# Ordering a recurrence's matmuls kind by kind over two batches: reads of both, values of both, state sums of both

## The chip, the cores and the metric

The kernel runs on one core of a Trainium2 chip. The metric is device time in microseconds (us), the median of several executions. TensorE multiplies matrices, VectorE, ScalarE and GpSimd do elementwise work, and SyncE issues the transfers. A ratio below is the mean time of one kernel's runs over the mean of the other's from the same rounds, so it is not quite the ratio of the medians quoted beside it.

## The reference

Four batches of eight heads go through a retention recurrence over 768 time steps; the result is the input of a two-layer network.

```python
gamma = 1.0 - 2.0 ** (-5.0 - np.arange(H))            # B, H, S, D = 4, 8, 768, 64
for t in range(S):
    state = gamma * state + outer(k[:, :, t], v[:, :, t])
    y[:, :, t] = scale * q[:, :, t] @ state
x = y.transpose(0, 2, 1, 3).reshape(B * S, H * D)     # 3072 x 512
h = x @ w_in                                          # 512 -> 2048
out = np.maximum(0.01 * h, h) @ w_out                 # 2048 -> 512
```

## The kernel before

The recurrence runs in six chunks of 128 steps. For one chunk and one batch there are two stages. The first makes the *scores* (keys against queries, `ap`), which VectorE masks. The second, shown here, has three kinds of product in one pair of PSUM banks: **reads** (queries against the state carried in), **values** (masked scores against values) and **state sums** (keys against values, for the next chunk). VectorE then drains the banks and updates the state.

```python
def stage_y(c, b, xb):                                # chunk c, batch b
    x, y = heads.pop((c, b)); ks, vs = y[:, 0], y[:, 1]
    am = scores.pop((c, b))
    ps = two_banks(f"yp_{c}_{b}")                     # 2 such buffers, shared with the scores
    pairs = [(j, m, i) for m in range(HP // 2) for j in range(2) for i in range(2)]   # eight
    if c > 0:
        for j, m, i in pairs:                         # reads: 64 rows x 64 columns of the array
            nc.tensor.matmul(ps[ts(i, 64), j, m, :], lhsT=st[b][ts(j, 64), 2 * m + i, :],
                             rhs=x[ts(j, 64), 0, 2 * m + i, :], start=(m == 0), stop=False, ...)
    for j, m, i in pairs:                             # values: 128 rows x 64 columns
        nc.tensor.matmul(ps[ts(i, 64), j, m, :], lhsT=vs[:, ...], rhs=am[:, j, 2 * m + i, :], ...)
    if more:                                          # state sums: 128 rows x 64 columns
        ...
    nc.vector.tensor_tensor(out=blocks, in0=ps[:, :, 0 : HP // 2, :], in1=gq, op=ALU.mult)  # drain
    if more:
        ...                                           # two VectorE operations: the new state
    load(...)                                         # the batch after the next
```

Around it lie the products of the feed-forward part (seven block products M1 to M7 in place of eight). In chunks 0 and 1 the batches are scored and read one by one, while the weights are still being loaded and rounded. In chunks 2 to 5 two batches are scored together behind one feed-forward product and read together three products later:

```python
at = {1: [scored(c + 1, u), scored(c + 1, u + 1)],
      4: [read(c + 1, u), read(c + 1, u + 1)]}
run(hidden(c, u, *xs[c], *pair[-1][1:]), at)
```

## Time and profile before

| | before |
|---|---|
| median of the first 3 runs | 688.67 us (688.64 to 690.79) |
| span of the profile | 686.5 us |
| TensorE busy | 663.5 us, 97% |
| VectorE, ScalarE, GpSimd busy | 55%, 24%, 4% |
| a paired stage with sums, without (chunk 5) | 4.17 us, 3.24 us |

A matmul's end in this profile is modelled and matmuls overlap. So "97% busy" says that TensorE nearly always has something running, not how fast. What a stretch of matmuls costs is read from the starts: from the first start of one stretch to the first start of the next. The prediction shows the lines.

### The profile page before, as it was taken

What the parts mean: (1) busy time and instruction counts of PE and PEld (TensorE: products, weight loads), DVE (VectorE), ACT (ScalarE), POOL (GpSimd) and SP (SyncE); (2) the same over time, 40 slices, a digit from 0 to 9 for tenths busy, and PEclk for the clock granted to TensorE, in tenths of its full rate; (3) what the DMA queues carried; (4) which work ended last, traced back from release to release, by engine and by line L of the source; (5) the groups of instructions that cost most, each with busy time, mean ns of one, the idle gap of its engine ahead of it and who ended that gap; (6) DMA issues with size and microseconds to landing.
All of it is one profiled execution on the core that took longest, in us unless ns stands there. A gap on an engine that the chain in (4) does not pass through costs nothing.

```text
span 686.5 us, 9550 instructions
## 1 busy us (share of the span) xinstructions
PE 663.5 (97%) x4096; PEld 578.9 (84%) x4096; DVE 375.6 (55%) x573; ACT 166.8 (24%) x275; POOL 28.0 (4%) x29
## 2 busy tenths in 40 slices
PE   5787999999999999999999999999999999999997
PEld 5676888888888888888888888888888888888886
DVE  4878767988888765613653533553451354341342
ACT  4432455445543001311210221220221130221210
POOL 1110000000001010100100100100000000000000
PEclk9999999999999999999999999999999999999999
DMA  8741222223412453100301300301300000100001
GB/s 315 283 154 62 82 72 84 92 72 123 153 34 90 138 181 119 55 1 10 114 1 62 123 0 1 123 1 62 123 0 1 1 1 16 46 1 0 1 1 62
DMA packets 15162, 49.12 MB, mean 72 GB/s; under 512 B 1680, under 2 KB 1680, under 8 KB 15120
## 3 DMA queue, kind: packets, MB, share of 16 engines
q1 hardware_dynamic: 15120, 48.51, 20.2%
q8 instruction: 32, 0.52, 0.3%
q14 instruction: 10, 0.08, 0.0%
HBM read 42.21 MB, written 6.29 MB: 71 GB/s over the span
## 4 chain that ended last, share of the span: by engine, by line
PE 94%; DMA 3%; DVE 1%; issue 1%; POOL 0%; ACT 0%; SPq 0%; POOLq 0%
PE B_h L303 12%; PE A_o L303 12%; PE B_o L303 12%; PE C_o L303 12%; PE C_h L303 12%; PE A_h L303 12%; PE D_h L303 6%; PE D_o L303 6%; PE yp L150 3%; PE ap L126 3%; PE yp L145 1%; PE yp L158 1%; DMA qk<-in_qk_dram 1%; DMA raw<-in_weights_dram 1%; DMA kv<-in_kv_dram 1%
## 5 line engine op out<-in xcount | busy, mean ns | idle before, releaser
L303 PE MATMUL A_h<-x,win 128*128 128x256 f32 x384 | 91.0, 380 | 0.0
L303 PEld LDWEIGHTS A_h<-x,win 128*128 128x128 f32 x384 | 72.7, 190 | 10.0
L303 PE MATMUL A_o<-g,wout 128*128 128x256 f32 x288 | 68.2, 380 | 0.0
L318 ACT ACTIVATE g<-g 128x512 f32<-128x512 f32 x72 | 43.8, 630 | 86.0 <-DVE g L252 85.9
L303 PEld LDWEIGHTS A_o<-g,wout 128*128 128x128 f32 x288 | 54.6, 190 | 7.8 <-ACT g L333 0.4
L252 DVE TENSOR_TENSOR m<-m,B_h 128x512 f32<-128x512 f32 x24 | 16.5, 687 | 65.6 <-PE B_h L303 65.6
L252 DVE TENSOR_TENSOR m<-m,B_o 128x512 f32<-128x512 f32 x16 | 11.0, 686 | 66.1 <-PE B_o L303 66.1
L323 ACT COPY m<-A_h 128x512 f32<-128x512 f32 x24 | 14.1, 586 | 135.6 <-PE A_h L303 103.9
L112 POOL TENSOR_TENSOR kv<-kv,dec 128x512 f32<-128x512 f32 x24 | 27.5, 1145 | 470.3 <-DMA kv<-in_kv_dram 276.8
L303 PE MATMUL B_h<-t,win 128*128 128x256 f32 x192 | 45.5, 380 | 1.0 <-DVE t L255 1.0
L303 PE MATMUL C_h<-t,win 128*128 128x256 f32 x192 | 46.1, 383 | 0.0
L303 PE MATMUL B_h<-x,win 128*128 128x256 f32 x192 | 46.0, 382 | 0.0
L303 PE MATMUL D_h<-t,win 128*128 128x256 f32 x192 | 45.5, 380 | 0.0
L303 PE MATMUL C_h<-x,win 128*128 128x256 f32 x192 | 45.5, 380 | 0.0
L163 DVE TENSOR_TENSOR x<-yp,dec 128x512 f32<-128x512 f32 x24 | 16.6, 690 | 46.3 <-PE yp L158 33.4
L303 PEld LDWEIGHTS B_h<-t,win 128*128 128x128 f32 x192 | 36.4, 190 | 6.3 <-DVE t L255 1.4
L150 PE MATMUL yp<-am,kv 128*64 128x128 f32 x384 | 29.4, 301 | 12.1 <-issue 8.1
L303 PEld LDWEIGHTS D_h<-t,win 128*128 128x128 f32 x192 | 36.4, 190 | 5.0
L303 PEld LDWEIGHTS C_h<-x,win 128*128 128x128 f32 x192 | 36.4, 190 | 5.0
L303 PEld LDWEIGHTS C_h<-t,win 128*128 128x128 f32 x192 | 35.9, 190 | 5.4
L303 PEld LDWEIGHTS B_h<-x,win 128*128 128x128 f32 x192 | 36.0, 190 | 5.3 <-issue 0.3
L255 DVE TENSOR_TENSOR gd<-g,gd 128x512 f32<-128x512 f32 x48 | 36.8, 767 | 1.6
(88 smaller groups left out, 1006.8 us busy)
## 6 DMA issues: line engine op xcount, KB each, us to landing
raw<-in_weights_dram SPq DMA_DIRECT2D x32, 512.0 KB, 3.8
qk<-in_qk_dram SPq DMA_DIRECT2D x24, 512.0 KB, 4.8
kv<-in_kv_dram SPq DMA_DIRECT2D x24, 512.0 KB, 5.5
out_dram<-o SPq DMA_DIRECT2D x24, 256.0 KB, 2.1
dec<-decay_dram SPq DMA_DIRECT2D x1, 262.0 KB, 5.5
```

Source lines behind the costliest of these rows:

```text
L112: nc.gpsimd.tensor_tensor(out=v, in0=v, in1=gk.unsqueeze(2).to_broadcast([128, H, D]), op=ALU.mult)
L126: nc.tensor.matmul(ps[:, j, a, :], lhsT=x[ts(j, 64), 1, a, :], rhs=x[ts(j, 64), 0, a, :])
L145: nc.tensor.matmul(ps[ts(i, 64), j, m, :], lhsT=st[b][ts(j, 64), a, :], rhs=x[ts(j, 64), 0, a, :], start=(m == 0), stop=False, skip_group_ ...
L150: nc.tensor.matmul(ps[ts(i, 64), j, m, :], lhsT=vs[:, 2 * a + j, :], rhs=am[:, j, a, :], start=(c == 0 and m == 0), stop=True, skip_group_ ...
L158: nc.tensor.matmul(sp[ts(j, 64), a, :], lhsT=ks[:, 2 * a + j, :], rhs=vs[:, 2 * a + j, :], start=False, stop=True, skip_group_check=True)
L163: nc.vector.tensor_tensor(out=blocks, in0=ps[:, :, 0 : HP // 2, :], in1=gq, op=ALU.mult)
L252: nc.vector.tensor_tensor(out=out, in0=a, in1=b, op=ALU.add)
L255: nc.vector.tensor_tensor(out=out, in0=a, in1=b, op=ALU.subtract)
L303: nc.tensor.matmul(ps[:, i, :], lhsT=block(w, sa)[:, k, ts(i, 128)], rhs=rhs[:, k, :], start=(first and i == 0 and n == 0 and k == 0), sto ...
L318: nc.scalar.activation(g[:, i], g[:, i], AF.Prelu, alpha=0.01)
L323: nc.scalar.copy(out=got["m1"], in_=ps)
```

## The change

The intent is to let products of one kind of both batches follow each other, so that TensorE meets fewer changes between kinds. The stage takes a tuple of batches. Its loops, cut to their order:

```diff
-    def stage_y(c, b, xb):
+    def stage_y(c, bs, xb):
+        got = [(b, *heads.pop((c, b)), scores.pop((c, b)), two_banks(f"yp_{c}_{b}")) for b in bs]
+        for b, x, _, _, ps in got:
             for ...:  # reads
+        for _, _, y, am, ps in got:
             for ...:  # values
+        for b, _, y, _, ps in got:
             for ...:  # state sums
+        for b, _, _, _, ps in got:
             # drain, state update, load
...
-                      3: [read(2, 2 * c), read(2, 2 * c + 1)]}
+                      3: [read(2, 2 * c, 2 * c + 1)]}
...
-                          4: [read(c + 1, u), read(c + 1, u + 1)]}
+                          4: [read(c + 1, u, u + 1)]}
```

Calls with one batch, in chunks 0 and 1, keep their order.

More of the change, by code (lines that the diff above doesn't have):

```diff
@@ L131, in stage_a @@
             in1=mask.unsqueeze(1).to_broadcast([128, H, C]), op=ALU.mult)
-    def stage_y(c, b, xb):
-        x, y = heads.pop((c, b))
-        ks, vs = y[:, 0], y[:, 1]
-        am = scores.pop((c, b))
-        ps = two_banks(f"yp_{c}_{b}")
-        pairs = [(j, m, i) for m in range(HP // 2) for j in range(2) for i in range(2)]
-        if c > 0:
-            for j, m, i in pairs:
-                a = 2 * m + i
+    def stage_y(c, bs, xb):
+        got = [(b, *heads.pop((c, b)), scores.pop((c, b)), two_banks(f"yp_{c}_{b}")) for b in bs]
+        more = c < NC - 1
+        pairs = [(j, m, i, 2 * m + i) for m in range(HP // 2) for j in range(2) for i in range(2)]
+        sums = {}
+        for b, x, _, _, ps in got:
+            for j, m, i, a in pairs if c > 0 else ():
                 nc.tensor.matmul(ps[ts(i, 64), j, m, :], lhsT=st[b][ts(j, 64), a, :],
@@ L147, in stage_y @@
                                  skip_group_check=True)
-        for j, m, i in pairs:
-            a = 2 * m + i
-            nc.tensor.matmul(ps[ts(i, 64), j, m, :], lhsT=vs[:, 2 * a + j, :],
-                             rhs=am[:, j, a, :], start=(c == 0 and m == 0), stop=True,
-                             skip_group_check=True)
-        more = c < NC - 1
-        if more:
-            sp = ps[:, 0, HP // 2 :, :].rearrange("p a (two d) -> p (a two) d", two=2)
-            for a in range(HP):
+        for _, _, y, am, ps in got:
+            for j, m, i, a in pairs:
+                nc.tensor.matmul(ps[ts(i, 64), j, m, :], lhsT=y[:, 1, 2 * a + j, :],
+                                 rhs=am[:, j, a, :], start=(c == 0 and m == 0), stop=True,
+                                 skip_group_check=True)
@@ L157, in stage_y @@
+        for b, _, y, _, ps in got:
+            sp = sums[b] = ps[:, 0, HP // 2 :, :].rearrange("p a (two d) -> p (a two) d", two=2)
+            for a in range(HP) if more else ():
                 for j in range(2):
-                    nc.tensor.matmul(sp[ts(j, 64), a, :], lhsT=ks[:, 2 * a + j, :],
-                                     rhs=vs[:, 2 * a + j, :], start=False, stop=True,
+                    nc.tensor.matmul(sp[ts(j, 64), a, :], lhsT=y[:, 0, 2 * a + j, :],
+                                     rhs=y[:, 1, 2 * a + j, :], start=False, stop=True,
@@ L160, in stage_y @@
                                      skip_group_check=True)
-        th, o = divmod(b * C, N)
-        blocks = xb.rearrange("p (kh th) k n -> p kh th k n", th=2)[:, :, th, :, ds(o, C)]
-        nc.vector.tensor_tensor(out=blocks, in0=ps[:, :, 0 : HP // 2, :], in1=gq, op=ALU.mult)
-        if more:
-            if c > 0:
-                nc.vector.tensor_tensor(out=st[b], in0=st[b], in1=sp, op=ALU.add)
-            nc.vector.tensor_tensor(out=st[b], in0=st[b] if c > 0 else sp,
-                                    in1=gc.unsqueeze(2).to_broadcast([128, HP, D]), op=ALU.mult)
@@ L169, in stage_y @@
-        n = c * B + b + AHEAD
-        if n < NC * B and n - 2 * B not in range(AHEAD):
-            load(*divmod(n, B))
+        for b, _, _, _, ps in got:
+            th, o = divmod(b * C, N)
+            blocks = xb.rearrange("p (kh th) k n -> p kh th k n", th=2)[:, :, th, :, ds(o, C)]
+            nc.vector.tensor_tensor(out=blocks, in0=ps[:, :, 0 : HP // 2, :], in1=gq, op=ALU.mult)
+            sp = sums[b]
+            if more:
+                if c > 0:
+                    nc.vector.tensor_tensor(out=st[b], in0=st[b], in1=sp, op=ALU.add)
+                nc.vector.tensor_tensor(out=st[b], in0=st[b] if c > 0 else sp,
+                                        in1=gc.unsqueeze(2).to_broadcast([128, HP, D]),
+                                        op=ALU.mult)
+            n = c * B + b + AHEAD
+            if n < NC * B and n - 2 * B not in range(AHEAD):
+                load(*divmod(n, B))
@@ L424, in scored, with read @@
         return do
-    def read(c, b):
-        return lambda: stage_y(c, b, xs[c][0])
+    def read(c, *bs):
+        return lambda: stage_y(c, bs, xs[c][0])
     def differ(c):
```

## The prediction

> **What bounds the kernel now.** I began with the page's first two parts, to see which engine sets the end.
>
> ```profile
> PE 663.5 (97%) x4096; PEld 578.9 (84%) x4096; DVE 375.6 (55%) x573; ACT 166.8 (24%) x275; POOL 28.0 (4%) x29
> ...
> PEclk9999999999999999999999999999999999999999
> ```
>
> TensorE is busy for 97% of 686.5 us at a clock that is nowhere throttled, and every other compute engine is under 60%. The chain that ended last says the same ("PE 94%; DMA 3%; DVE 1%"). So a change counts only if it alters the time TensorE needs, or makes it wait. The view of waits for TensorE says where it waits now:
>
> ```profile
> PE yp L150 <- issue: 8.1, 4, 4.6
> PE ap L126 <- DMA qk<-in_qk_dram: 5.7, 2, 4.6
> PE yp L150 <- POOL kv L112: 2.6, 2, 1.8
> PE yp L150 <- DVE am L129: 1.4, 1, 1.4
> PE B_h L303 <- DVE t L255: 1.0, 1, 1.0
> ```
>
> (Columns: total us, times, longest.) The same view restricted to 215 us onwards is empty: all these waits belong to the start, chunks 0 and 1, where the recurrence is done one batch at a time. The diff leaves those calls with one batch each, hence the same instructions. It pairs batches only in chunks 2 to 5, two pairs each: eight stages. In all eight TensorE waits for no other engine. Their durations come from the view by windows (us, then busy time of each engine):
>
> ```profile
> 229.68:233.85 4.17, 4.17 (x98) 3.69 (x97) 2.41 (x5) 0.00 (x0) 0.00 (x0) 1.00 0.54 150
> ...
> 433.37:437.55 4.18, 4.18 (x98) 3.70 (x97) 1.44 (x3) 0.60 (x1) 0.00 (x0) 1.00 0.47 136
> 488.27:491.52 3.25, 3.25 (x66) 2.56 (x65) 0.69 (x1) 0.60 (x1) 0.00 (x0) 1.00 0.45 141
> 542.24:545.49 3.25, 3.25 (x66) 2.56 (x65) 0.69 (x1) 0.60 (x1) 0.00 (x0) 1.00 0.00 0
> ```
>
> Six stages of 4.17 us and two of 3.25 us (chunk 5 has no state sums): 31.5 us, 4.6% of the span. That is all the change can work on. Inside one of them, the timeline (start, duration to the last end, engine, line, product, count):
>
> ```profile
> 433.37 0.67 PE L145 MATMUL yp<-qk,st 64*64 64x128 f32 x16
> 433.97 1.09 PE L150 MATMUL yp<-am,kv 128*64 128x128 f32 x16
> 434.90 0.63 PE L158 MATMUL yp<-kv 128*64 128x64 f32 x16
> 435.46 0.67 PE L145 MATMUL yp<-qk,st 64*64 64x128 f32 x16
> 436.06 1.09 PE L150 MATMUL yp<-am,kv 128*64 128x128 f32 x16
> 436.98 0.63 PE L158 MATMUL yp<-kv 128*64 128x64 f32 x16
> ```
>
> L145 is a state read (R), on a 64x64 corner of the array; L150 values (V) and L158 state sums (S) both use 128 rows and 64 columns. From start to start: R 0.60, V 0.92, S 0.56. The array changes shape at R to V and at S to R, but not at V to S. To price the seams I cut narrow windows around them:
>
> ```profile
> 433.75 0.29 PE L145 MATMUL yp<-qk,st 64*64 64x128 f32 x4
> 433.97 0.33 PE L150 MATMUL yp<-am,kv 128*64 128x128 f32 x2
> ...
> 435.30 0.23 PE L158 MATMUL yp<-kv 128*64 128x64 f32 x2
> 435.46 0.34 PE L145 MATMUL yp<-qk,st 64*64 64x128 f32 x4
> ```
>
> The last group of four reads starts at 433.75, the first pair of values 0.22 us later; the last pair of sums starts at 435.30, the next read 0.16 us later. (Reads start in fours within 0.02 us, values and sums in twos; I call these groups.) Inside a kind the instruction starts in the trace show 0.109 us from group to group for R and V, and 0.058 us for S. The first interval after a change of shape is also long: 0.160 us rather than 0.109, for R as for V.
>
> **What the Trainium skill says.** "TensorEngine Tiling (Array Packing)", Key Properties, says "Changing tiling mode (not just tile) drains the TensorE". The trace agrees: V to S, the same mode with another kind of product, goes on at V's own rhythm (last pair of values 434.79, first sums 434.90: 0.11 us), while both changes of mode cost extra. "TensorE: Matmul & The Clock Gate", section The mechanism, says that a weight load is pulled ahead of running matmuls when its row group doesn't conflict. In this trace loads do run ahead inside a kind, but the first loads of R and of V start only with their first matmuls (433.37 and 433.97 for both engine rows), which fits the long first interval. "Perfetto Trace Analysis", section Tensor Engine Instruction, says that a TensorE end is an estimate; so I use starts alone.
>
> **The change, part by part.** It adds and removes no matmul, vector operation or transfer. Before, the stage is R1 V1 S1 R2 V2 S2, after it R1 R2 V1 V2 S1 S2. One R to V seam and the S to R seam go; instead R meets R, V meets V and S meets S.
>
> *Removed seam R to V:* 0.220 between the groups' starts plus 0.160 for the first interval, where two ordinary intervals would take 2 x 0.109: 0.162 us over.
>
> *Removed seam S to R:* 0.158 instead of 0.058, plus 0.051 in the first interval: 0.151 us over.
>
> *New joints:* nothing extra, by this evidence. The scores (L126) already run two batches in a row here. Sixteen of them take 0.89 us from first to last start, as at 48.44; the 32 of a pair take 1.783 us, and their intervals are 0.112 us right through the joint between the batches, although a semaphore is waited on there.
>
> Check by adding up the whole new stage. Reads: 0.160 + 6 x 0.109 = 0.814 to the last group; 0.220 to values; values 0.160 + 14 x 0.109 = 1.686; 0.109 to sums; sums 0.056 + 14 x 0.058 = 0.873; 0.159 to the next feed-forward product (437.39 to 437.55). Sum 3.86 against 4.17: 0.31 us less. Chunk 5: 0.814 + 0.220 + 1.686 + 0.209 = 2.93 against 3.24: 0.315 less, since V to R costs what S to R does. Eight stages by 0.31 us: **2.5 us on the critical path, 0.36%**.
>
> *Moved, beside TensorE:* the first batch's drain and state update on VectorE (L163 0.69, L166 0.41, L167 0.42, together 1.56 us with gaps) now wait until the first batch's sums, which lie behind both batches' values. They start 3.5 us into the stage (2.83 to the sums, 0.41 for them, some 0.27 to the release) rather than 2.2. The second follows without a break and ends about 6.5 us in rather than 5.8. Relative to the end of TensorE's stage VectorE is then 1.1 us later. *Transfers:* the next keys and values can be fetched only after those sums, 1.3 us later for the first batch; the second batch's q and k are issued behind them on the same queue, also 1.3 us later.
>
> **The rivals.** *VectorE's backlog stalls TensorE.* For it: its work is bunched, and the differences of chunk 2's x follow the second drain directly, which a product needs at 259.50. Against it: in the stage at 433.37 VectorE waits 0.44 us for B_h straight after the drains, and TensorE has no wait there. In the tightest place (252.5) the difference needed is done near 257.1, some 2.4 us before its product; 1.1 us later still fits, unless GpSimd's decays, which already stretch one such operation from 0.7 to 1.25 us, collide more. Worth at most about 0.5 us: 686.7.
>
> *The later transfers become a wait.* For it: after the stage at 229.68 the scores come at 240.95, and the DMA engines are 74 to 100% busy from 231 to 239. Against it: a q/k load takes 4.8 us to land in the median (7.7 at most); issued at about 233.8 instead of 232.5 it is there by 239 to 241, and the scores of the second batch start near 241.5. All other pairs have 9 us or more. At worst 0.5 to 1 us, once: about 687.
>
> *Joints aren't free* (R2 and V2 wait on semaphores of their own, whose waiting instruction appears beside R's first loads, and the long first interval may belong to that rather than to the mode). If each new joint cost 0.05 us, 8 x 3 x 0.05 = 1.2 us of the gain would go: 687.4. Against it stands the scores' joint, and V, which has the same long interval without such an instruction.
>
> **Range and chances.** 688.67 - 2.5 = 686.2; with a small allowance for the first two rivals 686.3. The three runs of before spread by 2.15 us, as much as the gain. So the range is 685.3, all gained in a run as good as any, to 688.0, three quarters lost to joints or waits or to the spread. 2% would be 13.8 us; the eight stages are 31.5 us in all, so neither side is likely: faster 0.005, same 0.985, slower 0.01.
>
> **What would show it.** Right: paired stages of about 3.86 and 2.93 us; 32 reads in a row over 0.81 us from first to last start, 32 values over 1.69; no TensorE wait after 215 us; first drain some 3.5 us into the stage. Wrong: a paired stage still over 4 us, a jump of more than 0.11 us in the middle of a kind, or a TensorE wait on x, t or qk near 241 or 259 us.

## The result, and the profile after

| | before | changed |
|---|---|---|
| median of the 6 runs | 688.65 us (687.66 to 690.79) | 685.29 us (684.59 to 686.38) |
| ratio, 95% interval | | 0.9947 (0.9928 to 0.9966) |
| span of the profile | 686.5 us | 683.2 us |
| TensorE busy | 663.5 us | 660.3 us |

The time fell by half a percent, 0.01 us below the low end of the predicted range. The windows of the changed kernel, cut at the same stages (columns: window, its length, busy time of TensorE, weight loads, VectorE, ScalarE and GpSimd with counts, clock, DMA share, GB/s):

```profile
229.00:232.86 3.86, 3.86 (x97) 3.62 (x96) 1.32 (x3) 0.00 (x0) 0.00 (x0) 1.00 0.44 140
...
431.15:435.02 3.87, 3.87 (x98) 3.63 (x97) 0.35 (x1) 0.60 (x1) 0.00 (x0) 1.00 0.44 138
485.74:488.67 2.93, 2.93 (x65) 2.59 (x64) 0.69 (x1) 0.60 (x1) 0.00 (x0) 1.00 0.36 133
539.40:542.33 2.93, 2.93 (x65) 2.59 (x64) 0.69 (x1) 0.60 (x1) 0.00 (x0) 1.00 0.00 0
```

The stages have the 3.86 and 2.93 us that were worked out. The timeline of the changed kernel in the stage at 431 us (start, duration, engine, line, product, count):

```profile
431.15 1.10 PE L143 MATMUL yp<-qk,st 64*64 64x128 f32 x32
...
432.19 1.97 PE L148 MATMUL yp<-am,kv 128*64 128x128 f32 x32
...
433.99 1.10 PE L155 MATMUL yp<-kv 128*64 128x64 f32 x32
434.67 0.69 DVE L161 TENSOR_TENSOR x<-yp,dec 128x512 f32<-128x512 f32 x1 [7.31 <-PE yp L155]
```

Three stretches of 32 stand where six of 16 stood: 1.04 us of reads, 1.80 of values, 1.03 of sums, from start to start. VectorE's first drain (L161) starts 3.52 us into the stage, against 2.20 before. The one seam from reads to values that is left looks as both did before, in a narrow window:

```profile
431.97 0.29 PE L143 MATMUL yp<-qk,st 64*64 64x128 f32 x4
432.19 0.33 PE L148 MATMUL yp<-am,kv 128*64 128x128 f32 x2
```

Again 0.22 us. The view of waits for TensorE:

```profile
PE yp L148 <- issue: 7.3, 4, 4.6
PE ap L126 <- DMA qk<-in_qk_dram: 6.2, 3, 4.6
PE yp L148 <- DVE am L129: 2.7, 2, 1.4
PE yp L148 <- POOL kv L112: 1.5, 1, 1.5
PE B_h L303 <- DVE t L255: 1.0, 1, 1.0
```

From 215 us onwards this view is as empty as before: neither VectorE's later drains nor the later transfers became a wait. The waits that are left belong to the start-up and differ a little in size from those of before, with the same instructions; how often each occurs differs too (the wait for qk three times here, twice before).

To see where the 3.3 us between the two profiles lie, I cut both spans at chunk 2's first scores (behind which all eight paired stages lie) and at the start of the last value product:

| stretch | before | changed | difference |
|---|---|---|---|
| start to chunk 2's first scores ("start-up") | 222.31 us | 221.64 us | 0.68 us |
| to the start of the last value product | 322.97 us | 320.49 us | 2.48 us |
| to the end | 141.18 us | 141.10 us | 0.08 us |

The middle is what the prediction priced at 2.5 us; the eight stages alone add up to 31.52 us before and 29.04 us after. The start-up is where both programs hold the same instructions, with the same causes of waiting. In one pair of profiles 0.68 us there says little. Nor does it run at the full clock throughout, as two lines of the view by windows show for the kernel before (the clock is the third column from the end):

```profile
20.00:30.00 10.00, 7.47 (x88) 6.77 (x88) 8.29 (x14) 3.91 (x6) 2.01 (x2) 0.83 0.78 288
50.00:62.00 12.00, 6.66 (x105) 5.97 (x98) 10.64 (x16) 3.66 (x6) 1.58 (x1) 0.86 0.15 47
```

So the prediction's "at a clock that is nowhere throttled" is a misreading: in the row that it shows, a 9 stands for 90% or more of a slice of 17 us. The clock records of this trace have 3.41 us at half clock at 21.04 us and again at 55.17 us.

The experiments ask two things: is it the change of the array's shape that costs, and is the rest chance?

### The profile page after: what moved, and what is told of

Its sections match the earlier page's. It is cut to its first block, busy times and chain, and to the rows that moved or that the text cites. A ratio compares the mean times of both kernels' runs of the same rounds, so it can differ in the third digit from the quotient of the medians.

```text
span 683.2 us, 9545 instructions
## 1 busy us (share of the span) xinstructions
PE 660.3 (97%) x4096; PEld 577.8 (85%) x4096; DVE 375.9 (55%) x573; ACT 166.4 (24%) x275; POOL 27.4 (4%) x29
## 4 chain that ended last, share of the span: by engine, by line
PE 94%; DMA 2%; DVE 1%; issue 1%; POOL 0%; SPq 0%; POOLq 0%
PE B_h L303 12%; PE A_o L303 12%; PE B_o L303 12%; PE C_o L303 12%; PE C_h L303 12%; PE A_h L303 12%; PE D_h L303 6%; PE D_o L303 6%; PE ap L126 3%; PE yp L148 3%; PE yp L143 1%; PE yp L155 1%; DMA qk<-in_qk_dram 1%; DMA dec<-decay_dram 1%; DMA kv<-in_kv_dram 1%
## 5 line engine op out<-in xcount | busy, mean ns | idle before, releaser
L161 DVE TENSOR_TENSOR x<-yp,dec 128x512 f32<-128x512 f32 x24 | 16.5, 687 | 48.6 <-PE yp L155 36.3
L148 PE MATMUL yp<-am,kv 128*64 128x128 f32 x384 | 27.1, 295 | 11.5 <-issue 7.3
```

The costliest lines, as they stand in the source:

```text
L148: nc.tensor.matmul(ps[ts(i, 64), j, m, :], lhsT=y[:, 1, 2 * a + j, :], rhs=am[:, j, a, :], start=(c == 0 and m == 0), stop=True, skip_grou ...
```

## The experiments

Theory A: a change of the array's shape costs 0.15 to 0.16 us, joints within a shape cost nothing, and the rest of the difference is chance in the start-up. Its rivals: each change of the kind of product costs, whatever the shape; and the changed kernel also saves systematically outside the paired stages (theory B).

### The two kernels again

Kernel before, unedited:

> The kernel before, unedited, timed against itself, to see how far two groups of runs of one program lie apart. Theory A (the change gains 2.5 us in the eight paired stages and nothing else; the further 0.7 us between the two profiles, and the further 0.9 us between the medians, come from chance in the first 62 us, where both programs hold the same instructions): the ratio's interval holds 1, but the centre may be off by up to 0.0015 (1 us), the runs spread over 2 to 3 us, and in the profile the start of the long feed-forward run (61.85 us in the earlier profile of this kernel) moves by some tenths of a us to 1 us while the stages stay 4.17 and 3.24 us. Theory B (the start-up of the changed kernel is systematically shorter): this program's start-up stays within 0.2 us of 61.85 us.

Measured: 688.15 us against 688.69 for the same program in the same rounds, ratio 1.0003 (0.9985 to 1.0020). Stages 4.17 and 3.24 us; 322.97 us in the middle stretch to within 1 ns. The start-up ended at 222.20 us here, and the long feed-forward run started at 61.73 us, within the 0.2 us of 61.85 that theory B expected.

Changed kernel, unedited:

> The changed kernel, unedited, timed again. Theory A: 2.5 us less than before, 686.2 if before is 688.7; ratio 0.9964, with chance up to 0.0015 either way; paired stages 3.86 and 2.93 us again; the start of the long feed-forward run anywhere between 60.5 and 62.5 us. Theory B (a further saving in the start-up): ratio 0.995 or less again, and that start within 0.2 us of 61.12 us again.

Measured: 685.10 us against 688.69, ratio 0.9950 (0.9932 to 0.9968); middle stretch 320.49 us. The long feed-forward run started at 61.71 us where the first profile had 61.12. So a profile's start-up does wander, but the timed difference did not come down.

> The changed kernel a third time, because its two groups of runs so far were 3.4 us below before where the stages give 2.5. Theory A (chance in the start-up): over many runs the difference comes down towards 2.5, here between 1.5 and 3.5 us; the profile has 621.9 to 622.2 us from the start of the long feed-forward run to the end (before 624.6), and the start-up again lies anywhere between 61.0 and 63.5 us. Theory B (a systematic further saving of about 0.9 us before that point): 3.4 us again, and a start-up below 61.8 us again.

Measured: 685.46 us against 687.65, ratio 0.9965 (0.9945 to 0.9985), about the 2.5 us of theory A, and a start of the long run at 62.86 us, later than before's. Taken alone this would have closed the case for chance.

### Only the reads together

```diff
 reads of both
-values of both; state sums of both; drains of both
+for each batch: values, state sums, drain
```

> Only the reads of the two batches stand together: R1 R2 V1 S1 drain1 V2 S2 drain2. Theory A (only changes of the array's shape cost; S1 to V2 is the same shape): paired stages of 3.86 us and 2.93 us, as in the changed kernel (worked out: 0.814 + 0.220 + 0.814 + 0.109 + 0.405 + 0.058 + 0.763 + 0.109 + 0.405 + 0.159), so the same time as the changed kernel within 0.5 us, and the first drain starts some 2.8 us into the stage instead of 3.5. Rival (what costs is each change of the kind of product, so kind by kind is needed): three changes of kind more than one would have kind by kind, so some 0.1 to 0.15 us less gained for each of V1 S1 V2 S2's two further changes, stages of about 4.1 us, and 0.4 to 0.5 of the gain.

Measured: 685.80 us, ratio to before 0.9961 (0.9943 to 0.9978), stages 3.862 and 2.932 us. The timeline of this kernel:

```profile
432.92 1.10 PE L143 MATMUL yp<-qk,st 64*64 64x128 f32 x32
433.96 1.09 PE L148 MATMUL yp<-am,kv 128*64 128x128 f32 x16
434.88 0.64 PE L154 MATMUL yp<-kv 128*64 128x64 f32 x16
435.34 1.05 PE L148 MATMUL yp<-am,kv 128*64 128x128 f32 x16
436.22 0.64 PE L154 MATMUL yp<-kv 128*64 128x64 f32 x16
436.78 1.99 PE L300 MATMUL B_h<-x,win 128*128 128x256 f32 x8
...
435.56 0.69 DVE L159 TENSOR_TENSOR x<-yp,dec 128x512 f32<-128x512 f32 x1 [6.44 <-PE yp L154]
```

Values and sums alternate here, and the stage is as short as in the changed kernel (432.92 to 436.78). The step from the first batch's sums to the second's values has no break: 434.88 to 435.34 is 0.46 us for sixteen sums, where sums ahead of a change of shape take 0.56. So the change of kind costs nothing, and grouping the reads carries the whole gain of the stage. The first drain starts 2.64 us in instead of 3.52, as expected within 0.2 us.

### Only the sums together

```diff
-R1 V1 S1 R2 V2 S2, a drain behind each S
+R1 V1 R2 V2 S1 S2, both drains at the end
```

> Only the sums of the two batches stand together: R1 V1 R2 V2 S1 S2, drains after both. There are as many changes of shape as before (V1 to R2 takes the place of S1 to R2), but one change of kind fewer. Theory A: stages of 4.17 us (0.598 + 1.024 + 0.598 + 0.924 + 1.031 = 4.175) and 3.24 us, the time of before within 0.5 us plus chance. Rival (changes of kind cost): stages near 4.0 us and over 1 us gained. Rival (the later drains cost or gain something by themselves): a TensorE wait after 215 us, or a time 1 us or more off the kernel before.

Measured: 688.86 us, ratio 1.0007 (0.9986 to 1.0028), stages 4.174 and 3.244 us, no TensorE wait after 215 us. Two lines of the timeline:

```profile
435.54 1.09 PE L147 MATMUL yp<-am,kv 128*64 128x128 f32 x16
436.56 0.67 PE L143 MATMUL yp<-qk,st 64*64 64x128 f32 x16
```

Values ahead of reads take 1.02 us from start to start, where ahead of sums they take 0.92. One change of kind fewer gained nothing; late drains by themselves neither gain nor cost.

### More changes of shape

> The kernel before with more changes of shape, the same matmuls: in chunks 2 to 5 each batch's reads and values go in halves, R V R V S, which adds one V to R and one R to V change to each batch, four to a stage. Theory A (a change of shape costs 0.15 to 0.16 us over the ordinary interval): stages longer by 2 x (0.151 + 0.162) = 0.63 us, so 4.80 and 3.87 us, and 8 x 0.63 = 5.0 us more in all: 693.7 when before is 688.7, ratio 1.0073. Rival (drains and waits rather than shape set the time in the stages): the stages stay near 4.17 us.

This run missed its purpose. The kernel's list of pairs has eight entries, and I had split it at eight after counting sixteen records for each kind in the trace: each of these float32 matmuls leaves two matmul records. The program was that of before, and so served as a third repeat of it: 688.30 us, ratio 1.0009, stages 4.17 us. The mended edit:

```diff
-    if c > 0: reads(pairs)
-    values(pairs)
+    for some in (pairs[:4], pairs[4:]) if c > 1 else (pairs,):
+        if c > 0: reads(some)
+        values(some)
```

> The edit that d1_twice missed (its list of products has eight entries, so its two parts were all and none, and its program was that of before): the kernel before with the reads and values of chunks 2 to 5 in halves, R V R V S. Theory A (a change of shape costs 0.15 to 0.16 us over the ordinary interval): each batch gains one V to R (0.151) and one R to V (0.162), a stage 0.63 us: 4.80 and 3.87 us, 5.0 us in all; ratio to before 1.0073, and 328.0 us in the trace from chunk 2's first scores to the last value product, where before has 322.97. Rival (the seams' cost in the changed kernel is something else, such as a wait): the stages stay under 4.3 us.

Measured: 694.69 us against 689.12, ratio 1.0071 (1.0048 to 1.0094). The timeline of the first batch of one stage:

```profile
438.73 0.45 PE L145 MATMUL yp<-qk,st 64*64 64x128 f32 x8
439.11 0.66 PE L152 MATMUL yp<-am,kv 128*64 128x128 f32 x8
439.69 0.45 PE L145 MATMUL yp<-qk,st 64*64 64x128 f32 x8
440.07 0.66 PE L152 MATMUL yp<-am,kv 128*64 128x128 f32 x8
440.56 0.63 PE L165 MATMUL yp<-kv 128*64 128x64 f32 x16
441.12 0.45 PE L145 MATMUL yp<-qk,st 64*64 64x128 f32 x8
```

The stages take 4.795 and 3.867 us and the middle stretch 327.96 us: 4.99 us more than before for 32 more changes of shape, 0.156 us each, no wait involved. The changed kernel takes away 16 such changes and gains 2.48 us in the same stretch, 0.155 each. The two doses lie on one line.

All the changes of shape that were added or removed go to or from reads, so it could be the reads that cost, and not the shape. No run here separates the two, but seams without reads in the trace of the kernel before (after 215 us) do. Feed-forward products use 128x128 of the array and scores 64x128. A feed-forward product starts 0.158 us after the last sums, where sums follow each other in 0.058, and 0.208 us after the last scores, where scores follow each other in 0.112; scores start 0.309 us after the last feed-forward product, where these follow each other in 0.216. Each of the three also has a long first interval behind it. Seam and first interval together are 0.19 to 0.20 us over the ordinary ones, so a change of shape costs without reads too, and not always the same.

### Is the rest chance?

> The changed kernel a fourth time, beside e3_early. Theory A: the trace has 320.49 us from chunk 2's first scores to the last value product, as all its runs had (before 322.97), whatever the start-up takes; times some 2.5 us below before with chance of 1 us. Theory B (a systematic saving of 0.6 to 0.9 us more in the start-up): 3.2 us or more below before.

Measured: 685.05 us against 689.12, ratio 0.9941 (0.9919 to 0.9962), middle stretch 320.49 us again; this time the difference is the one of theory B. By then 24 runs of the changed kernel averaged 685.25 us and 51 of before 688.62, 3.4 us apart, where the steady stretches explain 2.5.

> The changed kernel a fifth time. The steady part (chunk 2's first scores to the end) is 461.58 us in all its traces and 464.1 us in those of before, so a run's span less that is its start-up: so far 221.93 us in the mean of 24 runs, against 222.74 in 45 runs of before. Theory A (chance): the start-up's mean here is nearer 222.7 than 221.9, and the difference to before in these rounds is near 2.5 us. Theory B (systematic): start-up 221.5 to 222.3 again, and 3.2 us or more below before.

Measured: 685.17 us against 688.56, ratio 0.9951 (0.9928 to 0.9973); start-up 222.04 us in the mean of six, again as theory B expected.

> The changed kernel with four GpSimd fills of the mask added at the very end, beside the last products: another program image with the same work and the same start-up instructions. If the short start-up came with that one program's image (where its instructions and data lie): start-up near 222.7, time 686.1. If it belongs to the order of the products, or is chance that holds on: near 221.9, time 685.3, or anything between.

```diff
+    for _ in range(4):
+        nc.gpsimd.memset(mask, 1.0)        # behind everything, unused
```

Measured: 685.20 us, ratio 0.9947 (0.9928 to 0.9967). Its trace has 461.11 us from chunk 2's scores to the end, so its start-up is 222.17 us, between the two values that were expected.

> The kernel before with the same four fills at the end. If images differ by chance: a start-up that may lie anywhere from 221.9 to 223.5. If the order of the late products decides: 222.7 again, and the time of before within 0.5 us.

Measured, with the same four lines: 688.11 us, ratio 0.9993 (0.9974 to 1.0012); 463.71 us to the end, start-up 222.76 us.

> r1_reads again: its steady part is that of the changed kernel (461.57 us) and its start-up was 222.35 us in the mean of six. Theory A: 222.0 to 223.0. Theory B in the form that fewer changes of shape shorten the start-up: 221.9, as in the changed kernel.

Measured: 685.57 us, ratio 0.9954 (0.9934 to 0.9974), start-up 222.19 us, in the range of theory A.

Each run records its span and its mean granted clock. A span less the length of the trace from chunk 2's scores to the end (461.58 us changed, 464.13 us before) is the run's start-up:

| program | runs | mean start-up |
|---|---|---|
| changed | 30 | 221.97 us |
| changed, padded | 6 | 222.17 us |
| only the reads together | 12 | 222.27 us |
| before | 56 | 222.73 us |
| before, padded | 6 | 222.76 us |
| only the sums together (464.48 us to the end) | 6 | 222.59 us |
| more changes of shape | 6 | 223.55 us |

The standard errors are 0.16 us for 30 runs, 0.17 for 56, 0.25 for 12 and 0.3 to 0.6 for six. Between changed and before it is 0.76 us, three times the error of the difference if all runs are taken as independent. In the four sets of rounds with both kernels it is 0.92, -0.13, 1.63 and 0.77 us, in the mean 0.80 with an error of 0.36, so just over twice. Part of the scatter goes with the granted clock: runs of before at 0.9935 or more have a start-up of 221.94 us, those at 0.9885 or less 223.47. The changed kernel had 3 of 30 runs in the low group, before 18 of 56. At equal clock its mean is still lower, 221.38 us in the high group and 222.40 against 222.87 in the middle one, but neither difference is twice its error (0.35 and 0.30 us). The padded pair differs by 0.6 us the same way, with an error of 0.5 us, so it neither shows nor rules out an accident of one program image. Pure chance, as I had expected, looks less likely than before, and is not excluded.

The traces show what the scatter goes with, though not the difference between the programs. At the start of chunk 2's scores the three traces of the kernel before stand at 222.31, 222.20 and 221.25 us, and the five of the changed kernel at 221.64, 222.05, 223.42, 221.39 and 222.43: no shorter. By the clock records, half clock comes there in stretches of 3.41 us or two or three times that. Of the 14 traces in which the start-up's code is unchanged, the six with 3.41 to 6.83 us of it have a mean start-up of 221.66 us, the eight with 13.65 to 17.07 us one of 223.22. What decides how many stretches a run gets, and what shortens the start-up of the changed kernel, if it is no chance, is **not settled**: in the traces the instructions there are the same, the waits vary from run to run of one program as much as between the programs, and I have no run that moves it at will.

### A version that beats both

The start-up still reads chunk 1's batches 2 and 3 one after the other. First I paired them too (`scored` makes the scores, `read` is the second stage, `round_piece` rounds a part of the weights, `differ` forms the differences of x that some products take):

```diff
-                for b in range(2, B):
-                    scored(1, b)(); round_piece(); read(1, b)()
-                differ(1)()
+                scored(1, 2)(); scored(1, 3)(); round_piece()
+                read(1, 2, 3)(); differ(1)(); round_piece()
```

> The changed kernel with one more pair: chunk 1's batches 2 and 3, which stand one after the other in the start-up, are scored together and read together (one batch of weight rounding moves behind the differences of x). There TensorE waited 4.8 us for the first batch's masked scores and 1.0 us for the second's, with cold clock in part. If the waits overlap: the start-up some 1 to 3 us shorter, time 682.3 to 684.3. Rival (VectorE is the bound there, busy 10.6 of 12 us, and does the same work): less than 0.8 us gained.

Measured: 685.02 us where the changed kernel had 685.46 in the same rounds, nothing clear, as the rival had it (less than 0.8 us gained). Then M1, which needs only batches 0 and 1, went in front of the paired read and M2 behind it:

> As e1_pair1, and the first hidden product of chunk 1 (M1, which needs the x of batches 0 and 1 alone) goes in front of the paired read, into TensorE's wait, with M2 right behind the read, as in chunk 0's first hidden unit. If TensorE's hole is filled: up to 1.7 us less than e1_pair1, 680.5 to 683. Rival (VectorE's chain sets when M6 can start, whatever stands before): the same time as e1_pair1 within 0.5 us.

Measured: 684.20 us, 1.3 us less than the changed kernel in the same rounds. TensorE still waited for the differences of x, the first of the two lines below; the second is the same product in the next experiment, which uses the order of the kernel with only the reads together:

```profile
64.44 2.12 PE L303 MATMUL B_h<-t,win 128*128 128x256 f32 x7 [1.91 <-DVE t L255]
```

```profile
65.08 1.99 PE L300 MATMUL B_h<-t,win 128*128 128x256 f32 x8 [0.98 <-DVE t L252]
```

> e2_fill's start-up with r1_reads' stage (reads together, then V1 S1 drain1 V2 S2 drain2). In e2_fill's start-up TensorE waited 1.9 us for the differences of x, whose chain on VectorE began with the first drain only after all of V1 V2 S1 S2, and VectorE had been idle 2.9 us before it. With the first drain in front of V2 the chain should start 1.0 to 1.5 us earlier and M6 with it: 683 us where e2_fill had 684.2, about 2 us less than the changed kernel in the same rounds; the late stages 3.86 and 2.93 us as before. Rival (the order of the drains makes no difference anywhere): the time of e2_fill within 0.5 us and a wait for t of 1.9 us again.

Measured: 682.62 us (681.58 to 684.15) against 685.05 for the changed kernel and 689.12 for before in the same rounds; ratio to before 0.9906 (0.9886 to 0.9927). The wait for t fell from 1.91 to 0.98 us. The step from the version before was timed in other rounds, but the two ratios to before don't overlap (0.9930 to 0.9966 there). In steady state the moment of the drains was free; in this start-up, where TensorE waits for VectorE's differences, drains in front of the second batch's values help. This version beats both kernels.

## Why the prediction was right or wrong

**The bound, and the stages the change can touch:** right. TensorE's own time set the gain, all of it in the eight paired stages as far as any trace shows.

**Removed seams:** right in mechanism and size. The sums gave 3.86 and 2.93 us a stage; measured 3.863 and 2.932. Priced at 0.151 and 0.162 us, the two seams measured 0.155 on average when removed and 0.156 when added.

**New joints free:** right; 32 reads take 0.835 us from first to last start (0.81 was worked out), and the stage comes out within 0.01 us. (One term of the prediction's check is not the sum written there: 0.056 + 14 x 0.058 is 0.868. The sums measured 0.873, at 0.0583 us an interval.)

**VectorE and the transfers later, but hidden:** right. The first drain starts 3.52 us into the stage, and there is no TensorE wait near 241 or 259 us, or anywhere after 215. The two rivals built on them fell, so the small allowance for them was not needed. Counted from the end of TensorE's stage, VectorE is done 0.9 us later than before, where 1.1 was worked out.

**"hence the same instructions":** this is the step that failed. I took the same instructions in chunks 0 and 1 for the same time, so the start-up's term in the sum was zero and had no spread of its own. The misread clock supported this: at a clock that is nowhere throttled, equal instructions might well take equal time, but the start-up has stretches at half clock, and in the eight traces of the two programs it takes 221.25 to 223.42 us. Over 30 and 62 runs the means are 685.27 and 688.63 us, 3.36 apart: 2.48 for the seams, 0.07 to the end (mean of the traces), and 0.8 left for the start-up. This remainder lies two to three errors from zero; that the change makes it is not shown, and its cause stays open. The first measurement, 3.36 us by the medians, had it in full.

**The range:** its low end, 685.3, allowed 0.9 us below the estimate of 686.2 for chance and nothing for a further effect, while single runs of one program spread over 3.8 us (changed) and 5.4 us (before); the median of six missed it by 0.01 us. Which side of the end a median of six falls on is partly luck: the four later ones of the changed kernel are 685.10, 685.46, 685.05 and 685.17 us, so four of five lie below. By my estimate from these spreads, a base of three runs calls for about a microsecond more on the low side. The chances (within 2%: 0.985) were right.

## What to carry to other kernels

Where small matmuls use parts of the array, count the changes of its shape and price one from the trace: the interval across the seam plus the long first interval behind it, less two ordinary intervals. Order the products so that those of one shape stand together, and don't regroup kinds that share a shape already; this leaves drains free to come early, which paid here in the start-up, where TensorE waited for another engine. And when the gain you look for is a few microseconds, take the traces' steady stretches for the mechanism, and many runs for the total: here they agreed on most of it but not on all. And look at the clock in the view by windows before you call a stretch equal in both programs.

## What the Trainium skill lacked or had wrong

- "TensorEngine Tiling (Array Packing)", Key Properties, says that a change of tiling mode drains TensorE, but not what that costs. Here a change between 64x64 and 128x64 cost 0.155 to 0.156 us over the ordinary interval, measured with 16 changes fewer and 32 more; going from one kind of product to another within 128x64 cost nothing measurable (stages of 3.862 and 3.863 us). A change into 128x128 or 64x128 took 0.19 to 0.20 us over.
- No page says how many matmul records a float32 matmul leaves in a profile: eight matmuls of the program left sixteen here.
- "TensorE: Matmul & The Clock Gate", section What's actually happening, says that the clock's activity window is free-running and so makes the first matmuls' speed vary from run to run. The runs agree that the start-up varies with the granted clock (221.94 us in the mean at 0.9935 or more, 223.47 at 0.9885 or less, kernel before), and the traces with 13.65 to 17.07 us of half clock in the start-up have a mean of 223.22 us there, those with 3.41 to 6.83 us 221.66. It does not tell why one program should get the low clock in 3 of 30 runs and another with the same start-up instructions in 18 of 56.
